# Per-head products on column halves of the array, moved in four batches behind another tiled unit

## The chip, the cores and the metric

One core of one Trainium2 chip. The metric is the device time of the kernel in microseconds (us). Before: 318.75 us, the median of four runs from 318.4 to 318.91.

## The reference

A linear attention feeds a gated feed-forward layer. Only the first part matters here: for each batch and head the product kv = softmax(k)^T v is a 64x64 matrix, and the attention output is softmax(q) times it.

```python
# q, k, v: (batch 8, heads 8, seq 576, head_dim 64)
q_s = softmax(q, axis=-1)
k_s = softmax(k, axis=2)                      # over the sequence
kv  = einsum('bhsd,bhse->bhde', k_s, v)       # 64x64 for each head
x   = einsum('bhsd,bhde->bhse', q_s, kv)      # -> (4608, 512)
out = (gelu(x @ w_gate) * (x @ w_val)) @ w_out
```

## The kernel before

TensorE works through the batches one after the other. For each it runs twelve groups of the first layer (`psg`, `psv`: 8 matmuls of 512 columns each, "FI 0" to "FI 11") and four blocks of output rows (`psy`: 12 matmuls each, "NS 0" to "NS 3"). The attention of the next batch rides in between, by a plan that says what follows which group: `at(b, FI, 5, ...)` puts work behind group 5 of batch b.

kv of two heads is one full-array product. Its 128x128 result has both heads' kv on the diagonal and two useless blocks beside it, which a mask sets to zero:

```python
    def kv_mm(b, g, j):
        # ... ps_att tile "pskv", two head pairs in it
        for n in range(NC):                                   # NC = 5 pieces of the sequence
            nc.tensor.matmul(
                st[(b, "pskv", g)][:, j, :], ek_b[b % 2][:, n, hp * P:(hp + 1) * P],
                v16_b[b % 2][:, n, 2 * hp:2 * hp + 2, 0:VW],  # 2 heads x 65: v and a column of ones
                start=(n == 0), stop=(n == NC - 1))

    def kv_norm(b, g):
        nc.vector.reciprocal(out=rck, in_=pskv[:, :, D])
        for j in range(2):
            nc.vector.scalar_tensor_tensor(out=kv_sb, in0=..., scalar=rck[:, j:j + 1],
                                           in1=mask, op0=ALU.mult, op1=ALU.mult)
```

For batches 3 to 7 the x unit (`unit_x4`) already works on 64x64 quarters of the array, with the heads in an order that suits it (heads c and c+4 share a pair). Batch 2 still takes x on the full array. The plan of batches 3 to 7:

```python
                at(b, FI, 5, L(unit_kv, n, 0))     # n = b + 1
                at(b, FI, 7, L(unit_kv, n, 1))
                at(b, NS, 1, L(unit_x4, n))
```

PSUM has six banks for matmuls (`ps_big`) and two for attention (`ps_att`).

The softmax here doesn't subtract the row's maximum and nothing guards it: scores larger than these inputs give would overflow.

## Time and profile before

| | before |
|---|---|
| time, median | 318.75 us |
| span of the profiled run | 316.7 us |
| TensorE busy | 309.7 us, 98% |
| VectorE / ScalarE / GpSimd busy | 195.4 / 138.4 / 44.6 us |
| kv, batches 1 to 7 | 140 matmuls of 130 columns, 1.15 us per batch |

In this document a matmul costs the distance from its start to the next one's, not its recorded duration; "by start times" means this. The prediction shows why, and reads the chain of waits.

### The profile page before, as it was taken

How to read it: one execution, taken by the hardware profiler on the slowest of the kernel's cores; microseconds unless marked ns; L12 is line 12 of the kernel's file. 1: busy time of each engine (PE TensorE's matmuls, PEld its weight loads, DVE VectorE, ACT ScalarE, POOL GpSimd, SP SyncE). 2: the span in 40 equal slices, each digit the busy share in tenths (PEclk: the TensorE clock that was granted, in tenths of full speed). 3: DMA queues.
4: the chain of work that ended last, by engine and by line, in shares of the span. 5: the costliest groups of instructions: out<-in, count | busy, mean ns of one | idle time of the engine just before them, and what ended most of it. 6: DMA issues, size and time to landing. Idle time of an engine off the chain costs nothing.

```text
span 316.7 us, 4572 instructions
## 1 busy us (share of the span) xinstructions
PE 309.7 (98%) x1698; PEld 146.8 (46%) x1698; DVE 195.4 (62%) x346; ACT 138.4 (44%) x179; POOL 44.6 (14%) x59
## 2 busy tenths in 40 slices
PE   8799999999999999999999999999999999999995
PEld 3444454455445444544444444444444444444444
DVE  3843386698898479847884689458953434234331
ACT  3753465989433663258233923392331233113300
POOL 2657551331003000110003000300000000000000
PEclk9999999999999999999999999999999999999999
DMA  7999999940196117821592149303020210140002
GB/s 229 372 383 395 400 386 388 394 174 0 68 321 236 45 66 251 291 56 68 169 364 63 55 122 382 97 10 132 3 63 23 91 42 2 27 105 2 2 33 99
DMA packets 42342, 50.76 MB, mean 160 GB/s; under 512 B 3408, under 2 KB 38096, under 8 KB 42320
## 3 DMA queue, kind: packets, MB, share of 16 engines
q1 hardware_dynamic: 40592, 48.84, 44.5%
q10 hardware_dynamic: 1728, 1.64, 1.6%
q8 instruction: 13, 0.21, 0.3%
q14 instruction: 9, 0.07, 0.1%
HBM read 37.75 MB, written 9.44 MB: 149 GB/s over the span
## 4 chain that ended last, share of the span: by engine, by line
PE 90%; DMA 4%; ACT 3%; DVE 2%; issue 1%; ACTq 0%
PE psy L471 29%; PE psg L393 28%; PE psv L393 28%; PE pskv L226 2%; DMA out_dram<-yo 2%; DMA qt<-in_q_dram 2%; PE psl L492 1%; DVE rq L190 1%; PE psx L365 1%; PE psx L347 1%; ACT eq L162 1%; PE pst L288 1%; DVE eq L199 0%; ACT L398 0%; ACT L162 0%
## 5 line engine op out<-in xcount | busy, mean ns | idle before, releaser
L398 ACT ACTIVATE gl<-psg 128x512 f32<-128x512 f32 x108 | 63.9, 598 | 141.4 <-PE psg L393 138.6
L400 DVE SCALAR_TENSOR_TENSOR ht<-psv,gl 128x512 f16<-128x512 f32 x108 | 72.9, 682 | 63.6 <-PE psv L393 63.0
L393 PE MATMUL psg<-xt,wg_sb 128*128 128x512 f16 x384 | 100.5, 379 | 0.1
L393 PE MATMUL psv<-xt,wv_sb 128*128 128x512 f16 x384 | 100.5, 379 | 0.0
L471 PE MATMUL psy<-wo_sb,ht 128*128 128x512 f16 x420 | 94.3, 379 | 0.0
L393 PEld LDWEIGHTS <-wv_sb 128*128 128x128 f16 x432 | 42.3, 98 | 51.2 <-issue 0.8
L393 PEld LDWEIGHTS <-wg_sb 128*128 128x128 f16 x432 | 41.6, 98 | 47.0 <-issue 0.4
L471 PEld LDWEIGHTS <-ht 128*128 128x128 f16 x420 | 40.4, 98 | 49.2 <-issue 2.1
L520 DVE TENSOR_SCALAR yo<-psy 128x512 f32<-128x512 f32 x30 | 20.6, 688 | 29.0 <-PE psy L471 29.0
L138 POOL CAST v<-vt 128x640 f16<-128x640 f32 x26 | 18.7, 761 | 137.5 <-DMA vt<-in_v_dram 92.2
L180 DVE TENSOR_REDUCE rq<-eq 128x10 f32<-128x640 f16 x28 | 22.7, 811 | 5.5 <-ACT eq L162 5.1
L199 DVE TENSOR_TENSOR eq<-eq,rrq 128x640 f16<-128x640 f16 (+1 forms) x29 | 23.4, 806 | 0.3
L162 ACT ACTIVATE ek<-kt 128x1280 f16<-128x1280 f32 (+1 forms) x11 | 19.1, 1746 | 3.4 <-DMA kt<-in_k_dram 3.4
L162 ACT ACTIVATE eq<-qt 128x2560 f16<-128x2560 f32 (+2 forms) x10 | 18.4, 1863 | 2.4 <-DMA qt<-in_q_dram 2.3
L313 DVE STREAM_TRANSPOSE et<-eq 128x640 f16<-128x640 f16 x20 | 16.9, 845 | 0.7
L140 ACT CAST xt<-psx 128x512 f16<-128x512 f32 x17 | 9.3, 589 | 7.4 <-PE psx L347 7.4
L393 PE MATMUL psg<-xtr,wg_sb 128*128 128x512 f16 x48 | 12.3, 379 | 0.0
L393 PE MATMUL psv<-xtr,wv_sb 128*128 128x512 f16 x48 | 12.3, 379 | 0.0
L385 PE MATMUL pswarm<-warm,ident 128*128 128x512 f16 x34 | 9.3, 430 | 1.4 <-POOL ident masks.py:199 1.4
L162 ACT ACT_TABLE_LOAD x8 | 10.3, 1283 | 0.7 <-DMA qt<-in_q_dram 0.6
L226 PEld LDWEIGHTS <-ek 128*128 128x128 f16 x140 | 9.1, 97 | 3.1
L142 DVE CAST xt<-psx 128x512 f16<-128x512 f32 x15 | 9.7, 681 | 1.2 <-PE psx L347 1.2
(70 smaller groups left out, 128.8 us busy)
## 6 DMA issues: line engine op xcount, KB each, us to landing
out_dram<-yo SPq DMA_DIRECT2D x14, 512.0 KB, 3.3
kt<-in_k_dram SPq DMA_DIRECT2D x7, 640.0 KB, 7.0
vt<-in_v_dram SPq DMA_DIRECT2D x7, 640.0 KB, 8.0
qt<-in_q_dram SPq DMA_DIRECT2D x7, 640.0 KB, 5.3
qt<-in_q_dram SPq DMA_DIRECT2D x8, 512.0 KB, 6.1
eqt<-et SPq DMA_DIRECT2D x80, 40.0 KB, 1.9
wost<-in_moe_w_out_dram SPq DMA_DIRECT2D x6, 512.0 KB, 7.9
kt<-in_k_dram SPq DMA_DIRECT2D x6, 512.0 KB, 7.5
```

What stands on the lines that cost most here:

```text
L138: nc.gpsimd.tensor_copy(out=dst, in_=src)
L142: nc.vector.tensor_copy(out=dst, in_=src)
L162: nc.scalar.activation(out=dst[:, n0:NC, h0 * D:h1 * D].rearrange(o, d=D, **({"t": 2} if b >= T32 else {})), in_=heads(tiles[(nm, b)], b, ...
L180: nc.vector.reduce_sum(rq, e, axis=mybir.AxisListType.X)
L199: (nc.gpsimd if eng == "pool" else nc.vector).tensor_tensor(out=e, in0=e, in1=rrq.unsqueeze(-1).to_broadcast((P, n, 2, D)), op=ALU.mult)
L226: nc.tensor.matmul(st[(b, "pskv", g)][:, j, :], ek_b[b % 2][:, n, hp * P:(hp + 1) * P], v16_b[b % 2][:, n, 2 * hp:2 * hp + 2, 0:VW], start ...
L313: nc.vector.transpose(out=et[:, :, hp].rearrange("p c (n i) -> p n c i", i=32), in_=eq_b[b % 2][:, :, hp * P:(hp + 1) * P].rearrange("p n ...
L393: nc.tensor.matmul(ps, w[:, ci, fi * P:(fi + 1) * P], xt[:, ci, :], start=(ci == 0), stop=(ci == HP - 1))
L398: nc.scalar.activation(out=gl, in_=psg, func=ACTF.Gelu)
L400: nc.vector.scalar_tensor_tensor(out=ht, in0=psv, scalar=_H_SCALE, in1=gl, op0=ALU.mult, op1=ALU.mult)
L471: nc.tensor.matmul(psy, hts[fi][:, ns * P:(ns + 1) * P], wo_sb[:, fi, :], start=(fi == 0), stop=(fi == NFI - 1))
L520: nc.vector.tensor_scalar(out=yo, in0=psy, scalar1=1.0 / _H_SCALE, scalar2=None, op0=ALU.mult)
```

## The change

The intent is to make only the diagonal blocks: each head's product takes one column half of the array (128 rows by 64 columns), two heads run at once, and no mask is needed. Batch 2 gets the head order and the tiled x unit of the later batches. For batches 4 to 7 kv follows the x unit of the batch before, which is tiled already, ahead of the last block of output rows.

```diff
+    QUAD = 2                      # head order of the tiled units: from batch 2 (was T32 = 3)
...
+    def unit_kv4(b):
+        ps = ps_att.tile([P, HP, VW], f32, name="pskv", tag="att")
+        for hp in range(HP):
+            for n in range(NC):
+                for s in range(2):
+                    c0 = hp * P + s * D
+                    nc.tensor.matmul(
+                        ps[s * D:(s + 1) * D, hp, :], ek_b[b % 2][:, n, c0:c0 + D],
+                        v16_b[b % 2][:, n, 2 * hp + s, 0:VW], start=(n == 0), stop=(n == NC - 1))
+        rck = att.tile([P, HP], f32, name="rck4", tag="rck4")
+        nc.vector.reciprocal(out=rck, in_=ps[:, :, D])
+        kv = att.tile([P, HP, D], f16, name="kv4", tag="kv4")
+        nc.vector.tensor_tensor(out=kv, in0=ps[:, :, 0:D],
+                                in1=rck.unsqueeze(-1).to_broadcast((P, HP, D)), op=ALU.mult)
...
-    at(1, NS, 0, L(unit_trem, 2), L(unit_kv, 2, 0))
-    at(1, NS, 1, L(unit_x, 2, 0, "dve"))
-    ... (five more pieces of kv and x of batch 2)
+    at(1, NS, 0, L(unit_trem, 2))
+    at(1, NS, 1, L(unit_kv4, 2))
+    at(1, NS, 2, L(unit_x4, 2, ("dve", "dve")))
...
-                at(b, FI, 5, L(unit_kv, n, 0))
-                at(b, FI, 7, L(unit_kv, n, 1))
-                at(b, NS, 1, L(unit_x4, n))
+            if n == T32:                            # batch 3
+                at(b, FI, 5, L(unit_kv4, n))
+            at(b, NS, 2, L(unit_x4, n))
+            if n + 1 < B:
+                at(b, NS, 2, L(unit_kv4, n + 1))
```

More of the change, by code (lines that the diff above doesn't have):

```diff
@@ L98 @@
     wo_sb = wpool.tile([P, NFI, C], f16, name="wo_sb")
+    QUAD = 2
     T32 = 3
     def heads(x, b, h0, h1):
-        if b >= T32:
+        if b >= QUAD:
             return x.rearrange("p (t c) x -> p c t x", t=2)[:, h0 // 2:h1 // 2]
@@ L159, in exp @@
         dst = (ek_b if nm == "k" else eq_b)[b % 2]
-        o, i = (("p n (c t d) -> p c t n d", "p c t (n d) -> p c t n d") if b >= T32 else
+        o, i = (("p n (c t d) -> p c t n d", "p c t (n d) -> p c t n d") if b >= QUAD else
                 ("p n (h d) -> p h n d", "p h (n d) -> p h n d"))
         nc.scalar.activation(
-            out=dst[:, n0:NC, h0 * D:h1 * D].rearrange(o, d=D, **({"t": 2} if b >= T32 else {})),
+            out=dst[:, n0:NC, h0 * D:h1 * D].rearrange(o, d=D, **({"t": 2} if b >= QUAD else {})),
             in_=heads(tiles[(nm, b)], b, h0, h1)[..., n0 * D:NC * D].rearrange(i, d=D),
@@ L167, in cast_v @@
     def cast_v(b, h0, h1, eng="pool"):
-        if h1 - h0 > 2 and (eng == "pool" or b >= T32):
+        if h1 - h0 > 2 and (eng == "pool" or b >= QUAD):
             for h in range(h0, h1, 2):
@@ L172, in cast_v @@
         copy_on(eng, v16_b[b % 2][:, :, h0:h1, 0:D].rearrange("p n h d -> p h n d"),
-                (tiles[("v", b)][:, h0 // 2::4] if b >= T32 else tiles[("v", b)][:, h0:h1]).rearrange(
+                (tiles[("v", b)][:, h0 // 2::4] if b >= QUAD else tiles[("v", b)][:, h0:h1]).rearrange(
                     "p h (n d) -> p h n d", d=D))
@@ L274, in unit_kv @@
         kv_norm(b, g)
+    def unit_kv4(b):
[12 more added lines that the diff above has]
+                                in1=rck.unsqueeze(-1).to_broadcast((P, HP, D)), op=ALU.mult)
+        st[(b, "kv4")] = kv
     def get_eqt(b):
@@ L356, in unit_xrem, with unit_x4 @@
         copy_on(eng, xtr[:, :, b * REM:(b + 1) * REM], psx)
-    def unit_x4(b):
+    def unit_x4(b, engs=("act", "dve")):
         xt = get_xt(b)
@@ L364, in go @@
                 r, t = slice(64 * s, 64 * s + 64), hp % 2
-                nc.tensor.matmul(ps[s][64 * t:64 * t + 64], st[(b, "kv", hp)][r, s, :], src[r],
+                nc.tensor.matmul(ps[s][64 * t:64 * t + 64], st[(b, "kv4")][r, hp, :], src[r],
                                  start=True, stop=True)
@@ L370, in unit_x4 @@
             go([p[:, hp // 2] for p in psr], hp, xqr(b, hp))
-        for s, eng in enumerate(("act", "dve")):
+        for s, eng in enumerate(engs):
             copy_on(eng, xtr[:, 2 * s:2 * s + 2, b * REM:(b + 1) * REM], psr[s])
@@ L376, in unit_x4 @@
                 go(ps, hp, xq(b, hp))
-            for s, eng in enumerate(("act", "dve")):
+            for s, eng in enumerate(engs):
                 copy_on(eng, xt[:, i + 2 * s, :], ps[s])
@@ L620 @@
     at(1, FI, 11, L(load_batch, 3), L(exp, "k", 2, 4, 8), L(exp, "q", 3), L(exp, "k", 3), L(exp_rem0), L(cast_v, 3, 0, H))
-    at(1, NS, 0, L(unit_trem, 2), L(unit_kv, 2, 0))
-    at(1, NS, 1, L(unit_x, 2, 0, "dve"))
-    at(1, NS, 12, L(unit_kv, 2, 1))
-    at(1, NS, 2, L(unit_x, 2, 1, "dve"), L(unit_x, 2, 2, "dve"))
-    at(1, NS, 13, L(unit_x, 2, 3, "act"))
-    at(2, FI, 0, L(unit_xrem, 2, "dve"))
+    at(1, NS, 0, L(unit_trem, 2))
+    at(1, NS, 1, L(unit_kv4, 2))
+    at(1, NS, 2, L(unit_x4, 2, ("dve", "dve")))
     at(2, FI, 7, L(norm_rem0))
@@ L635 @@
             n = b + 1
-            if n < T32:
-                at(b, FI, 0, L(norm, n, 0))
-                at(b, FI, 1, L(unit_kv, n, 0))
-                at(b, FI, 2, L(norm, n, 1))
-                at(b, FI, 3, L(unit_kv, n, 1))
-                at(b, FI, 4, L(unit_t, n, 0), L(norm, n, 2))
-                at(b, FI, 6, L(unit_x, n, 0), L(norm, n, 3))
-                at(b, FI, 7, L(unit_x, n, 1))
-                at(b, FI, 8, L(unit_t, n, 1))
-                at(b, FI, 9, L(unit_trem, n))
-                at(b, FI, 10, L(unit_x, n, 2), L(unit_x, n, 3))
-                at(b, FI, 11, L(unit_xrem, n))
-            else:
-                for hp in range(HP):
-                    at(b - 1, NS, hp, L(norm_sum, n, hp))
-                    at(b, FI, hp, L(norm_mul, n, hp), L(unit_t32, n, hp))
-                at(b, FI, 4, L(moves, n))
-                at(b, FI, 5, L(unit_kv, n, 0))
-                at(b, FI, 7, L(unit_kv, n, 1))
-                at(b, NS, 1, L(unit_x4, n))
+            for hp in range(HP):
+                at(b - 1, NS, hp, L(norm_sum, n, hp))
+                at(b, FI, hp, L(norm_mul, n, hp), L(unit_t32, n, hp))
+            at(b, FI, 4, L(moves, n))
+            if n == T32:
[3 more added lines that the diff above has]
+                at(b, NS, 2, L(unit_kv4, n + 1))
     def ride(b, kind, i):
```

## The prediction

> **What bounds the kernel now.** I read the page first: busy shares, then the chain that ended last.
>
> ```profile
> PE 309.7 (98%) x1698; PEld 146.8 (46%) x1698; DVE 195.4 (62%) x346; ACT 138.4 (44%) x179; POOL 44.6 (14%) x59
> ...
> PE 90%; DMA 4%; ACT 3%; DVE 2%; issue 1%; ACTq 0%
> ```
>
> TensorE is busy 98% of 316.7 us and carries 90% of the chain. A busy share alone would not prove it, since a matmul is recorded as 379 ns although its successor starts 216 ns later. So I looked at the chain in order of time for one batch, where each row is the time until the next step.
>
> ```profile
> 128.19 0.86 PE psv L393 x4
> 129.06 0.57 PE pskv L226 x10
> 129.63 0.86 PE psg L393 x4
> ...
> 133.08 0.57 PE pskv L226 x10
> ...
> 140.91 5.18 PE psy L471 x24
> 146.09 0.19 PE psxr L365 x8
> 146.27 0.43 PE psx L365 x8
> 146.71 5.29 PE psy L471 x24
> 151.99 0.86 PE psg L393 x4
> ```
>
> Nothing but TensorE stands here and the rows join: 0.86 us for 4 matmuls of 512 columns is 216 ns each[...]. From batch 2 on the end is therefore set by the sum of what is streamed through the array. A matmul removed there shortens the run by its whole cadence, as long as no wait takes its place.
>
> The change touches two rows of it. The kv of one batch is two groups of 10 matmuls, 128 rows by 128 columns, 130 moving columns. By their start times 57.5 ns lie between two, and 575 ns are spent per group, so 1.15 us per batch. The second is the x unit on 64x64 quarters, which batches 3 to 7 already use:
>
> ```profile
> 145.71 0.38 PE L471 MATMUL psy<-wo_sb,ht 128*128 128x512 f16 x1
> 146.02 0.26 PE L365 MATMUL psxr<-eqt,kv_sb 64*64 64x64 f16 x8
> 146.10 0.61 PE L365 MATMUL psx<-eqt,kv_sb 64*64 64x512 f16 x8
> 146.64 0.61 PE L471 MATMUL psy<-wo_sb,ht 128*128 128x512 f16 x2
> ```
>
> This timeline is the only place where the kernel before already runs tiles, so it is my measuring stick. The last full matmul starts at 145.707 and streams 216 ns, to 145.923; the first quarter starts at 146.016. That is 93 ns to enter the mode. The 16 starts of the unit, read one by one in ns from its first: 0, 3, 7, 10; 52, 56, 60, 62; 84 to 94; 303 to 313. So four quarters start within 10 ns and run together, two of them on the same rows and different columns. The last four start at 313 and stream 216 ns; the next full matmul starts 93 ns later and its successor comes 10 ns late: 103 ns to leave. Together the unit costs 725 ns (all five are within 2 ns of it), of which 196 ns are the two switches.
>
> **What the Trainium skill says.** "TensorEngine Tiling (Array Packing)", section Key Properties: changing the tiling mode drains the array. The trace agrees, with 93 ns in and 103 out. The same page, section Restrictions of its tile mapping: column tiling disables Fast Weight Load. That is the danger, since a kv matmul brings its own weights. In the trace the loads of the second round start at 26 ns, and its matmuls at 52; the loads of the third start at 55, right after the matmuls of the second, and its matmuls at 84. So a load of 64 columns takes 26 to 29 ns, and the third round's load ran under the second round's matmuls. Here the trace contradicts "TensorE: Matmul & The Clock Gate", section "The mechanism", by which a weight load overlaps matmuls in flight only when the row group differs: these are the same rows. Its section "Wait — 56ns, not 53.3ns?" gives a floor of about 25 ns from start to start however small a matmul. The 20 one-column matmuls of the k sums agree (25 ns, full array); the quarters, 3 to 4 ns apart, don't, so I take the floor to hold per tile and not over tiles.
>
> **The change part by part.**
>
> *kv on column halves.* 20 matmuls of 130 columns become 40 of 128 rows by 64 columns and 65 moving columns. Half of the old products lay off the diagonal and were masked away; they are no longer made. Two halves should run together, so there are 20 rounds. A round takes the longer of 65 columns (scaled from 57.5 ns for 130 columns: about 29 ns) and a 64-column load (26 to 29 ns); the quarters' last short round took 32 ns. I take 31 ns: 20 x 31 = 620 ns, plus 26 ns for the first load, which nothing hides, plus 93 ns to enter: 740 ns.
>
> *Batches 4 to 7.* kv follows x directly, so the leaving switch of x becomes kv's and only one switch more is paid. I assume that quarters to column halves costs as much as full array to quarters, 93 ns. 1150 - 740 = 410 ns each, 1.64 us for four.
>
> *Batch 3.* kv stands alone among the first-layer matmuls and pays the leaving as well: 740 + 103 = 843 ns, 0.31 us saved.
>
> *Batch 2.* kv stands alone: 0.31 us saved. Its x goes from four full matmuls of 512 columns and four of 64 (4 x 216 + 4 x 29 = 980 ns) to the unit of 725 ns: 0.255 us saved.
>
> *VectorE.* Per batch, two reciprocals (155 ns) and four masked products (347 ns each), 1.7 us, become one reciprocal and one product over 128x256, which I size at 0.41 us by the 128x256 cast. This lies beside TensorE and gains nothing by itself.
>
> *The move.* x goes from after the second block of output rows to after the third. No work is added.
>
> Sum: 1.64 + 0.31 + 0.31 + 0.255 = 2.5 us of 318.7, to 316.2. That is 0.8%.
>
> **The rivals.**
>
> *The halves are limited by issue or loads, not by columns.* kv then needs 80 instructions in a row behind the 32 of x, more than any burst of small ones in this trace. If the 25 ns of the k sums hold for each matmul and not for each tile, kv takes 40 x 25 = 1.0 us, plus 119 ns on entering: nothing gained in batches 4 to 7, and only x of batch 2 is, against 0.1 us lost in each kv that stands alone: about 318.5. For: the k sums are the only small matmuls of which a run of ten is seen, and no stretch here tells how fast the sequencer refills its queue. Against: 16 matmuls and their loads start in 94 ns and two rounds of 16 in about 300. If loads did not hide under matmuls at all, a round takes 57 ns and the time is the same as this. I give both together one chance in six.
>
> *A wait takes the place of the gain.* (a) kv needs a PSUM slot of the pair that x has just used; it comes free with ScalarE's first copy, which takes 0.24 us and starts about 0.3 us after x. That ends near 0.55 us, and x streams to 0.53 and switches to 0.62. So at most some 50 ns a batch, 0.2 us in all. (b) kv of batch n+1 needs its exp and the cast of v. In the batch shown, the exp of k ends at 146.43 (ScalarE's timeline) and the cast of v at 135.8, where kv would start near 149.4: 3 us of slack. (c) The first layer needs x copied. After the move 0.74 us of kv and 2.6 us of the last rows lie between. VectorE needs 0.6 for the rows' eviction, 0.2 and 2 x 0.6 for its copies, some 2.2 us after x began, and 4.1 are there. (d) In batch 2 all six copies are on VectorE: rows 0.6, two short ones 0.4, four long ones 2.4, so the last ends some 3.6 us after the third block, against 3.3 us to the first matmul of batch 2 and 4.0 to the one that reads the last copied chunk. It fits by 0.3 us, and the first gate comes over 1 us later than now, with three PSUM pairs to absorb it. If it doesn't, batch 2 loses up to 0.4 us.
>
> *The switch between two tiled modes is free,* since the column division stays: 4 x 93 ns more, to about 315.8. Nothing in this trace shows it, for it has only one tiled mode.
>
> **Range and chances.** The main path gives 316.2; free switches and 29 ns rounds would give 315.7; small waits of (a) and (d) 316.8; the issue rival 318.5. Weighing the tail a little I put 316.3, with 315.6 to 317.6 for eight in ten. Two per cent is 6.4 us. All kv there is costs 8 batches x 1.15 = 9.2 us and most of it must stay, so faster by that much is all but excluded. Slower by it needs over 1 us lost in each of six batches. Runs of before spread over 0.5 us, which does not blur this.
>
> **What would show it.** In the profile after, the chain's kv row should be one piece of 40 matmuls: about 0.74 us behind x and in batch 3 about 0.84 with the leaving. Single starts should come in pairs 3 to 4 ns apart, pairs 29 to 32 ns apart, with about 93 ns from the last x stream to the first kv matmul. The pskv share of the chain, 2% now, should fall by about a third. TensorE should wait for no copy of x at the starts of batches 2 to 7 and for no ScalarE copy ahead of kv. Starts 25 ns apart or more within a pair would mean that the issue rival holds, and pairs 57 ns apart that loads don't hide. An unbroken gap before the first gate of batch 2 would mean (d).

## The result, and the profile after

316.25 us, the median of four runs from 315.97 to 316.4; the ratio to before is 0.9922, with a 95% interval of 0.9905 to 0.9939. Ratios here are the mean time of one kernel's fast runs over that of the other's of the same rounds, so not quite the ratio of the medians quoted. The gain is 2.5 us or 0.8%, clear of noise.

The page of the changed kernel, busy time and chain by engine:

```profile
PE 307.7 (98%) x1826; PEld 143.7 (46%) x1826; DVE 191.1 (61%) x324; ACT 138.5 (44%) x178; POOL 44.7 (14%) x59
...
PE 90%; DVE 4%; DMA 2%; ACT 2%; issue 1%; ACTq 0%; DVEq 0%
```

128 more matmuls, 2 us less of TensorE, still the bound. The chain in order of time through the same stage as before (start, duration, engine, tile, line, count):

```profile
131.79 0.86 PE psv L411 x4
132.65 0.86 PE psg L411 x4
...
139.90 7.77 PE psy L489 x36
147.67 0.18 PE psxr L383 x8
147.85 0.43 PE psx L383 x8
148.29 0.75 PE pskv L284 x40
149.04 2.69 PE psy L489 x12
151.73 0.86 PE psg L411 x4
```

The two kv pieces of 0.57 us are gone from the first layer. One piece of 0.75 us stands behind x, and the rows join without a wait. The last 12 `psy` matmuls take 2.69 us instead of 2.59, because the leaving of the tiled mode is counted with them; before, the same 0.1 us was in the 5.29 us behind x.

TensorE's timeline at that place, with shapes:

```profile
147.60 0.26 PE L383 MATMUL psxr<-eqt,kv 64*64 64x64 f16 x8
147.68 0.60 PE L383 MATMUL psx<-eqt,kv 64*64 64x512 f16 x8
148.22 0.82 PE L284 MATMUL pskv<-v,ek 128*64 128x65 f16 x40
148.97 0.60 PE L489 MATMUL psy<-wo_sb,ht 128*128 128x512 f16 x2
```

The 40 starts, read one by one in ns from the first: 0, 3; 53, 56; 88, 92; 118, 121; 148, 151; 183, 187; ... 593, 598; 623, 627. Pairs 0 to 8 ns apart, mostly 3 or 4, rounds 29 to 36 ns apart, and a first gap of 53: the second pair's weight load begins at 27, its matmuls only 26 later. Entering the tiled mode is counted from the end of the stream before (216 ns after the start of a matmul of 512 columns). Three numbers make up a kv, and six kv in the first profile give them within a few ns:

| | entering | first start to the next full matmul | its successor late by | less the leaving, paid before too | kv costs | before | saved |
|---|---|---|---|---|---|---|---|
| behind x (batches 4 to 7) | 88 to 90 ns | 755 | 10 | 103 | about 753 | 1150 | about 397 |
| alone (batches 2, 3) | 93 to 94 ns | 755 | 10 | - | about 859 | 1150 | about 291 |

The x of batch 2 costs 725 ns, as the unit did before in the other batches, so 255 ns less. Together: 4 x 397 + 2 x 291 + 255 = 2.43 us.

The profile also has something that nobody asked for. The two profiled spans differ by 2.2 us. The last matmul starts 2.20 us earlier; 0.09 of that is a quicker start of the program, so the rest is 2.11, and 0.3 us is missing against 2.43. It stands in the transposes of batch 2, TensorE's timeline at 70.6 us. Before, then after:

```profile
70.69 0.61 PE L288 MATMUL pst<-ident,eq 128*128 128x128 f16 x8
```

```profile
70.61 0.86 PE L306 MATMUL pst<-ident,eq 128*128 128x128 f16 x7
```

After the fourth transpose a gap of 0.30 us opens (the second answer ends before the eighth). VectorE's timeline tells what they waited for: the last product that normalises q of batch 2. Before, then after:

```profile
69.92 0.92 DVE L199 TENSOR_TENSOR eq<-eq,rrq 128x640 f16<-128x640 f16 x1
```

```profile
69.85 1.23 DVE L200 TENSOR_TENSOR eq<-eq,rrq 128x640 f16<-128x640 f16 x1
```

That product takes 0.82 us elsewhere (the mean of its 27 in the profile before is 815 ns). The change does not touch it. The experiments come back to it.

### The profile page after: what moved, and what is told of

The parts are those of the page before. It is cut to its first block, busy times and chain, and to the rows that moved or that the text cites. A ratio compares the mean times of both kernels' runs of the same rounds, so it can differ in the third digit from the quotient of the medians.

```text
span 314.5 us, 4799 instructions
## 1 busy us (share of the span) xinstructions
PE 307.7 (98%) x1826; PEld 143.7 (46%) x1826; DVE 191.1 (61%) x324; ACT 138.5 (44%) x178; POOL 44.7 (14%) x59
## 4 chain that ended last, share of the span: by engine, by line
PE 90%; DVE 4%; DMA 2%; ACT 2%; issue 1%; ACTq 0%; DVEq 0%
PE psy L489 29%; PE psg L411 28%; PE psv L411 27%; DMA qt<-in_q_dram 2%; PE pskv L284 1%; DVE eq L200 1%; PE psl L510 1%; PE psx L383 1%; DVE rq L191 1%; DVE rq L181 1%; DVE ht L418 1%; PE psx L365 1%; ACT eq L163 1%; PE pst L306 1%; ACT L416 0%
## 5 line engine op out<-in xcount | busy, mean ns | idle before, releaser
L141 ACT CAST xtr<-psxr 128x128 f16<-128x128 f32 (+1 forms) x6 | 1.7, 283 | 17.8 <-PE psxr L383 17.8
```

Source lines behind the costliest of these rows:

```text
L141: nc.scalar.copy(out=dst, in_=src)
```

## The experiments

My theory going in: TensorE's stream is the bound, two column halves run at once, and following x saves one leaving of the tiled mode. Rivals: the gain comes from the move; it comes from narrower matmuls alone; an issue limit holds over tiles; batch 2's share is eaten by its six copies on VectorE.

Span comparisons below are taken from the start times in the profile where an effect is smaller than the run-to-run noise of about 0.5 us. They leave out the stall at 70.8 us, which came and went between executions, and how early the program got going (the first kv starts between 13.25 and 13.93 us).

**e1_again: the changed kernel once more.**

> The changed kernel once more, unaltered: the reference for the other runs of this call, and a second profile. 316.2 us, 2.5 us under before. In the first profile TensorE stood 0.30 us inside the transposes of batch 2 (at 70.8 us), behind a normalising product on VectorE that took 1.23 us instead of 0.82 while GpSimd cast v. If the change causes that stall, it is here again at about 0.3 us. If it is a matter of phase between the two engines, its size differs here (0 to 0.5 us).

Measured 316.19 us, ratio 0.9920 (0.9907 to 0.9934). The stall was there again, with 0.40 us. So the time repeats. What the stall is, this run does not tell.

**e2_old_place: halves without the move.**

```diff
-            if n == T32:
-                at(b, FI, 5, L(unit_kv4, n))
-            at(b, NS, 2, L(unit_x4, n))
-            if n + 1 < B:
-                at(b, NS, 2, L(unit_kv4, n + 1))
+            at(b, FI, 5, L(unit_kv4, n))
+            at(b, NS, 1, L(unit_x4, n))
```

> kv on column halves, but in its old place in the first layer for all of batches 3 to 7, and x in its old place. My theory: only the leaving of the tiled mode is paid once more for each of batches 4 to 7, so 4 x 0.10 = 0.4 us over the changed kernel: 316.7. Each kv alone costs 0.86 us from the last full matmul's stream to the regular rhythm. Rival, that following x directly is what brings the gain: back to about 318.2.

Measured 316.43 us, ratio 0.9928 (0.9915 to 0.9940), against 316.19 for the changed kernel on the same chip. The chain in the first layer of this run:

```profile
127.27 0.86 PE psv L411 x4
128.14 0.75 PE pskv L284 x40
128.89 0.97 PE psg L411 x4
```

The kv piece is as long as behind x, and the leaving shows in the 0.97 us of the next four matmuls, 0.86 otherwise. By start times, the span is 0.41 us longer than that of the changed kernel without its stall: 4 leavings of 0.103 us, as expected. The times show 0.24 us, which their intervals cannot tell from 0.4 or from 0. The rival that following x brings the gain falls: the move is worth a sixth of it.

**e3_move_only: the move without halves.**

```diff
-                at(b, FI, 5, L(unit_kv, n, 0))
-                at(b, FI, 7, L(unit_kv, n, 1))
-                at(b, NS, 1, L(unit_x4, n))
+                if n == T32:
+                    at(b, FI, 5, L(unit_kv, n, 0))
+                    at(b, FI, 7, L(unit_kv, n, 1))
+                at(b, NS, 2, L(unit_x4, n))
+                if n + 1 < B:
+                    at(b, NS, 2, L(unit_kv, n + 1, 0), L(unit_kv, n + 1, 1))
```

(on the kernel before)

> The move alone: kv of batches 4 to 7 follows x, x after the third block of rows, but kv stays on the full array with masked products, as before; batch 2 as before. My theory: the same columns are streamed, 1.15 us per kv, and nothing is gained: 318.7, as before. The chain shows kv as 0.57 us for 10 matmuls, twice, behind x. Rival, that the gain is from taking kv out of the first layer (a lighter VectorE there): 317 or less.

Measured 318.6 us, ratio 0.9995 (0.9982 to 1.0007): nothing gained. The chain behind x:

```profile
149.40 0.43 PE psx L365 x8
149.83 1.25 PE pskv L226 x20
151.09 2.59 PE psy L471 x12
```

1.25 us is the 1.15 of a kv and the leaving of 0.10. A move of work within a stream that has no gaps changes nothing unless it saves a switch.

**e4_same_half: the loops exchanged.**

```diff
-            for n in range(NC):
-                for s in range(2):
+            for s in range(2):
+                for n in range(NC):
```

> The changed kernel with the loops of kv exchanged: the five matmuls of one column half follow one another, then the five of the other, the same 40 matmuls and the same result. My theory, that the gain is two halves at once: only the seven changes of half overlap, 33 steps of 31 ns, so about 1.02 us of stream instead of 0.62; 0.4 us more in each of six batches, 2.4 us in all: 318.6, and up to 319.9 if nothing overlaps. Rival, that the gain is from narrower matmuls and no masked-off columns alone: 316.2 as before. The issue floor of 25 ns per matmul, if it held over tiles, would give the same time too.

Measured 316.64 us, ratio 0.9936 (0.9922 to 0.9950). My expectation of 318.6 was wrong, and not because the theory of two halves was: the edit did not take the overlap away. The chain:

```profile
148.03 0.43 PE psx L383 x8
148.47 0.81 PE pskv L284 x39
149.28 2.70 PE psy L489 x12
```

Only 0.06 us longer per kv. The starts, in ns: 0, 53, 58, 88, 111, 118, 147, 148, 176, ... 688. On a single half matmuls are 29 to 36 ns apart (the run e11 below: 0, 53, 89, 118, 148), so the first five, which are all of one half in the program, need about 148 ns. Here six have started by 118. Some of the second five must have overtaken. The packed trace also shows an overtaking directly: the matmul that waits on a semaphore, the first of the second pair of heads and so the eleventh of the program, starts as the eleventh in all six kv of the changed kernel, and here as the tenth in all six, at 183 or 184 ns. In four of them the tenth of the program is marked too, by the semaphore that it raises; it starts 22 or 23 ns after the eleventh. The order of the program within that burst hardly matters, and I had counted on it.

**e11_one_half: the overlap really taken away.**

```diff
-        ps = ps_att.tile([P, HP, VW], f32, name="pskv", tag="att")
+        for s in range(2):
+            ps = ps_att.tile([P, HP, VW], f32, name="pskv", tag="att")
...
-                        ps[s * D:(s + 1) * D, hp, :], ...
+                        ps[0:D, hp, :], ...
...
+            nc.vector.reciprocal(out=rck[0:D], in_=ps[0:D, :, D])
+            nc.vector.tensor_tensor(out=kv[s * D:(s + 1) * D], in0=ps[0:D, :, 0:D], ...)
```

> The changed kernel with all 40 matmuls of a kv on the first column half: heads c in one PSUM tile, heads c+4 in a second one on the same partitions; VectorE brings the second to its partitions with a second reciprocal and product, the result stays right. In the run with exchanged loops the two halves overlapped all the same (40 starts in 685 ns), so it did not take the overlap away; this does. My theory, that the gain comes from two halves at once: a matmul every 30 to 33 ns on one half, 40 x 31.5 = 1.26 us instead of 0.655, so 0.6 us more in each of six batches: 3.6 us over the changed kernel, 319.8. Rival, that halves save only by streaming fewer columns and would be as fast one after the other: 316.2.

Measured 319.75 us, ratio 1.0031 (1.0019 to 1.0044): slower than the kernel before. The result was right.

```profile
150.00 0.43 PE psx L383 x8
150.43 1.38 PE pskv L285 x40
151.81 1.40 PE psy L489 x6
```

1.38 us in place of 0.75, 0.63 more, six times: 3.8 us, which is also what the start times add over the changed kernel. The same number of matmuls, of columns and of loads. VectorE's added work is no rival: the starts within a kv are 29 to 36 ns apart after the first gap, and none waits. So two halves at once is the gain; 40 narrow matmuls in a row would have been a loss. It also says what the masked-off columns were worth: nothing, since a full-array matmul of 130 columns (57.5 ns) costs no more than two halves in a row (63 ns).

**e6_kv_twice: a kv without any switch.**

```diff
-                at(b, NS, 2, L(unit_kv4, n + 1))
+                at(b, NS, 2, L(unit_kv4, n + 1), L(unit_kv4, n + 1))
```

> The changed kernel with kv of batches 4 to 7 done twice in a row (the second takes the place of the first, the result is the same). It measures a kv without any switch of mode: 20 rounds of 31 ns, 0.63 us, so 4 x 0.63 = 2.5 us over the changed kernel: 318.7. If instead the queue runs dry in a long burst of small matmuls (80 of them and as many loads), the second kv takes over 1.0 us: 320.2 or more.

Measured 318.8 us, ratio 1.0009 (0.9995 to 1.0022).

```profile
148.37 0.43 PE psx L383 x8
148.81 1.39 PE pskv L284 x80
150.19 2.70 PE psy L489 x12
```

By start times, the second kv adds 633 ns, 31.7 ns a round. The 80 matmuls and 80 loads run at the same rate from first to last: no sign of a queue that runs dry.

**e5_batch2_old: batch 2 as before.** The edit puts back the old plan of batch 2 and `QUAD = 3`.

> The changed kernel with batch 2 as before (full-array kv and x, six rows in four places), all else as changed. My theory: batch 2's share of the gain is 0.29 us for kv and 0.255 us for x, so 0.55 us is given back: 316.8. Rival, that the six copies on VectorE hold up the first gate of batch 2 and eat the gain: 316.2 or less.

Measured 316.87 us, ratio 0.9949 (0.9937 to 0.9962). By start times 0.54 us over the changed kernel, the stalls left out on both sides. Batch 2 gives its share, and its six copies on VectorE hold nothing up: the trace of the changed kernel has no gap of over 20 ns in TensorE's stream from that x to the next kv, but for the leaving of the tiled mode.

**e7_kv3_behind_x2: kv of batch 3 behind x of batch 2 too.**

```diff
-    at(1, NS, 2, L(unit_x4, 2, ("dve", "dve")))
+    at(1, NS, 2, L(unit_x4, 2), L(unit_kv4, 3))
...
-            if n == T32:
-                at(b, FI, 5, L(unit_kv4, n))
```

> A version that might be better: kv of batch 3 directly behind x of batch 2 as well, and the copies of that x on ScalarE and VectorE in turn, as in the later batches. One entry from full array to tiles and one leaving (0.19 us) become one switch between tiled modes (0.09 us): 0.10 us under the changed kernel, 316.1, which the profile shows and the times hardly do. Rival: kv waits for a PSUM slot or ScalarE is still busy with exp, and it is the same or slower.

Measured 316.53 us, ratio 0.9944 (0.9932 to 0.9957): no gain, and by start times some 0.4 us lost. The first kv behind x in the timeline of all engines:

```profile
82.18 0.61 PE L383 MATMUL psx<-eqt,kv 64*64 64x512 f16 x8
...
82.21 0.69 DVE L538 TENSOR_SCALAR yo<-psy 128x512 f32<-128x512 f32 x1 [1.07 <-PE psy L489]
...
82.82 0.28 DVE L143 CAST xtr<-psxr 128x128 f16<-128x128 f32 x1
...
83.24 0.35 PE L284 MATMUL pskv<-v,ek 128*64 128x65 f16 x11 [0.45 <-ACT xt L141]
```

kv started 614 ns after x's stream instead of 90. The view names a ScalarE copy as the releaser, the last that ended. But the compiled program makes this kv wait for VectorE as well, as none of the later ones does, and TensorE's queue passes a semaphore at 83.14, just after VectorE's short copy ended at 83.10. That copy stands behind the eviction of output rows.

**e8_late_transposes: the waiting transposes later.**

```diff
-    at(1, FI, 10, L(unit_t, 2, 1))
-    at(1, FI, 11, L(load_batch, 3), ...)
+    at(1, FI, 11, L(unit_t, 2, 1), L(load_batch, 3), ...)
```

> The changed kernel with the second half of batch 2's transposes one first-layer group later (after the twelfth instead of the eleventh). If the stall of TensorE at 70.8 us in the changed kernel's first profile is due to the late product on VectorE, it is gone, and the time is up to 0.3 us under the changed kernel: 315.95. Rival: the late VectorE holds TensorE up elsewhere, at the same cost: 316.2.

Measured 316.11 us, ratio 0.9927 (0.9914 to 0.9939). The times can't tell 315.95 from 316.2; the profile shows the rival. In it the product took 1.40 us, the transposes did not wait, and the first layer did instead: 0.42 us, for a PSUM bank that the late VectorE had not emptied.

```profile
70.60 1.03 PE L411 MATMUL psg<-xt,wg_sb 128*128 128x512 f16 x4
71.89 0.59 PE L411 MATMUL psv<-xt,wv_sb 128*128 128x512 f16 x2 [0.26 <-DVE ht L418]
```

**e12_v3_later: the cast of v out of the way.** The ten profiles so far, before and after included, let me line up GpSimd's four casts of v of batch 3 with the product on VectorE; e11, which ran beside this one, makes them eleven.

```diff
-            (nc.scalar if b == 0 and t == 1 else nc.sync).dma_start(
+            (nc.scalar if b == 0 and t == 1 or (nm, b) == ("v", 3) else nc.sync).dma_start(
...
-    at(1, FI, 11, L(load_batch, 3), L(exp, "k", 2, 4, 8), L(exp, "q", 3), ...)
+    at(1, FI, 11, L(load_batch, 3, ((q, "q"), (k, "k"))), L(exp, "k", 2, 4, 8),
+       L(exp, "q", 3), L(load_batch, 3, ((v, "v"),)), ...)
```

> The changed kernel with v of batch 3 loaded later (issued by ScalarE behind the exp of q, about 78 us, instead of at 61), so that GpSimd does not cast it while VectorE makes the last normalising product of batch 2 at 69.8 us. Theory: that product ran long because it waited for a cast in flight; here it takes 0.82 us, TensorE has no stall at 70.8, and the time is 0 to 0.4 us under the changed kernel, 316.0. Rival: the product is long for another reason and stays at 0.9 to 1.4 us.

Measured 316.18 us, ratio 0.9916 (0.9903 to 0.9930). The casts came at 78.1 us, the product took its normal time, and the stall was gone:

```profile
69.75 0.83 DVE L200 TENSOR_TENSOR eq<-eq,rrq 128x640 f16<-128x640 f16 x1
```

In eight of the eleven profiles with the early load, the product started while a cast had 0.25 to 0.69 us to run, and in e8 just 6 ns before a cast. In these nine the product ended 670 to 678 ns after that cast did, whenever it had started itself (in the profile after: cast to 70.397, product to 71.071; before: 70.173 and 70.845). In the other two, e2 and e6, the cast in flight had only 83 ns left, and the product came ahead of the next one, by 26 and 27 ns. It took 0.83 us, and the cast begun behind it took 1.38 us instead of 0.72. Either engine waits for nearly the whole of the other's instruction (some 0.15 us of the later one's usual time lies under the recorded end of the earlier). The Trainium skill says so in "SBUF — State Buffer", section "SBUF: two separate sides": VectorE and GpSimd share a pair of ports by "an **exclusive lock**, not a bandwidth split", and a VectorE operation with two SBUF inputs needs it against a GpSimd operation that reads SBUF. The trace agrees, with the numbers above, but for those 0.15 us. How much the product loses, from nothing to 0.6 us, is a matter of which comes first and by how much. In seven profiles of kernels whose code up to there is that of the changed one (e8 not counted) the transposes stood 0.30, 0.40, 0.34, 0.29 and 0.43 us in five and not at all in two (e2, e6). With the old batch 2 (before, e3, e5) it was 0, 0.05 and 0.19. Three against seven do not settle whether the change makes it likelier; that stays open. The times of e1 and e12, 316.19 and 316.18 in different rounds, show no gain from its absence, so whether the 0.3 us of single profiles is in the medians is not shown either.

**e13_best: both together.** As e12, and as e7 with both short copies of x of batch 2 on ScalarE.

> Both together: v of batch 3 later, and kv of batch 3 behind x of batch 2 with both short copies of that x on ScalarE (in the earlier try kv stood 0.52 us behind VectorE's short copy, which came after an eviction of rows). Without that wait kv starts 90 ns after x's stream; 0.10 us gained there and up to 0.4 at the transposes: 315.9. Rival: another wait takes its place and it is 316.2 or more.

Measured 316.38 us, ratio 0.9921 (0.9907 to 0.9935). In the profile it does what it should:

```profile
82.11 0.43 PE psx L383 x8
82.55 0.75 PE pskv L284 x40
83.30 2.69 PE psy L489 x12
```

kv starts 90 ns after x's stream, which bears out VectorE's short copy as the wait of e7 (the load of v moved too, but its cast had ended by 72 us in e7), and by start times the span is 0.10 us shorter than that of e12 (whose first kv started 0.21 us earlier, so that the recorded spans show the opposite). The times don't show it: 0.1 us is below what five rounds resolve. No version here measurably beats the changed kernel.

## Why the prediction was right

316.3 was predicted, 316.25 measured, and the steps hold one by one. That the two agree to 0.05 us is partly luck: runs of one kernel spread over some 0.4 us, and a stall that was not foreseen stands in single profiles.

- *TensorE's stream sets the end.* Shown: in e6 four kv of 633 ns more lengthened the time by 2.6 us over e1 (of other rounds), in e11 six times 0.63 by 3.6 over e12.
- *Two halves at once.* Shown by e11, which on TensorE takes only that away and loses 3.6 us.
- *A round of 31 ns.* 31.7 in e6 as a mean; single rounds are 29 to 36 ns, where 29 to 32 was forecast. The loads hide under the matmuls: unhidden ones would have made it 57 by the prediction's sum.
- *740 ns behind x.* About 753. The term that was short is the rounds (20 x 0.7 = 14 ns), while entering took 88 to 90 ns instead of 93.
- *843 ns alone.* About 859 in batches 2 and 3, for the same reason.
- *A switch between two tiled modes costs as much as one from the full array.* 88 to 90 against 93 ns. The rival of a free switch falls.
- *x of batch 2.* 725 ns in the trace, as assumed; e5 gives 0.54 us for kv and x of batch 2 where 0.565 was summed.
- *The sum.* 2.43 us where 2.5 was summed.
- *Waits.* None took the place of the gain in the changed kernel: no kv waits for a bank, no first layer for a copy. (d), the tight one, fitted: the last of the six copies ended at 85.61 us, 3.67 us after the third block where 3.6 was reckoned, and no first-layer matmul waited for it.
- *The issue rival* falls with the starts in pairs and with e6. Two readings in its paragraph were wrong, without effect on the forecast. By 99 ns twelve quarters had started, not sixteen by 94. And loads that don't hide would not give "the same" time: 20 x 57 + 93 ns is 0.11 us more per kv than the 40 x 25 + 119 beside it, 0.7 us in all.

What the prediction did not have is the stall of 0.3 us at 70.8 us in the profile after. The product ran long before the change too (0.92 us), and whether the change lengthens it is open. And my picture of how overlap comes about was too narrow: e4 showed that the order of the two halves in the program is not what makes them overlap.

## What to carry to other kernels

When TensorE is the bound and a product has useless blocks, splitting it over array halves pays only if both halves stream at once: look at the start times for pairs, not at busy time. Put tiled units next to each other; each return to the full array cost 0.1 us here and each entry 0.09, which for a unit of 0.65 us is nearly a third on top. Before moving a unit ahead of another, ask which engine empties the bank it will take, and what that engine has in front of it.

## What the Trainium skill lacked or had wrong

- "TensorE: Matmul & The Clock Gate", "The mechanism": its list has a weight load overlap matmuls in flight only with a different row group, although the paragraph above the list also lets a load into the background weight buffer go ahead. Here all loads use all rows, and a round of load and matmul takes 31.7 ns, hardly more than the 65 columns alone (an estimate of 29, half of 57.5). The list's "only" is too strong; the prediction read the list without the exception.
- The same section has matmuls start in strict program order. In e4 the eleventh matmul of the program started before the tenth, by 22 or 23 ns in the four kv where both are marked, and 40 took 0.69 us against 1.26 on one half: matmuls of one column half overtake those of the other.
- The same page's floor of about 25 ns from start to start is stated without limit. Over tiles it does not hold: 40 matmuls in 627 ns, pairs mostly 3 or 4 ns apart, close to the 4 ns between tiles that the page itself draws further down. On one half, e11 never goes below 29 ns.
- "TensorEngine Tiling (Array Packing)", "Key Properties", says that a change of mode drains the array, without a number: 93 ns from full array to tiles, 88 to 90 from quarters to column halves, 103 back to the full array.
- "TensorEngine Tiling (Array Packing)", "Restrictions", says that column tiling disables the fast load, but not what that costs. Here, with 65 columns to stream, it can be little: a round took 31.7 ns, against an estimate of 29 for the columns alone. Whether the fast load was on before is not shown.
